# Attention and a GELU feed-forward in one planned kernel: shifted copies on GpSimd, two more bit buffers, new planning tables

## The chip, the cores and the metric

The kernel runs on one core of a Trainium2 chip. The core has five engines with queues of their own: TensorE (PE; its weight loads are shown as PEld), VectorE (DVE), ScalarE (ACT), GpSimd (POOL) and SyncE (SP, which here only issues DMAs). They share the on-chip memory; the matmul results lie in eight banks of their own ("ps"), which GpSimd does not use in this kernel. The metric is the device time of one execution in microseconds (us); lower is better.

## What is computed

A transformer block over 2048 tokens of width 640, in bf16: layer norm, attention with 32 query heads of width 20 that share one key head and one value head, a residual, a second layer norm, a gated feed-forward of width 1536, and a second residual.

```python
q = (x @ wq).reshape(B, S, H, Dh)          # H = 32, Dh = 20
k = x @ wk                                  # one head for all
v = x @ wv
scores = jnp.einsum("bhqd,bkd->bhqk", q, k) * (Dh ** -0.5)
p = softmax(scores)
o = jnp.einsum("bhqk,bkd->bhqd", p, v)
...
h = x + attention(layernorm(x))
y = layernorm(h)
out = h + (gelu(y @ w_gate) * (y @ w_up)) @ w_down
```

## The kernel before, in words

**Tiles and passes.** The tokens are 16 tiles of 128. A tile's 32 heads are done in two halves, so there are 32 passes. A pass needs the scores of 16 heads against 16 key tiles. One *unit* is one key tile against four heads that lie in one quarter of the partitions, a bank of 128 x 512; a pass has 64 units, the kernel 2048. Four units of one key tile make a *quad*.

**Two ways to the exponential.** Most units are done on ScalarE (L979): a group of three or two banks is turned into exponentials in one instruction, written to one of five `pbuf` slots, and multiplied by the values (L1093, `pbuf`, `v_ext`). Some quads of each pass, as many as the digit of `D_QUADS`, are done on VectorE instead. There a "bit product" (L933) adds a bias to the score and writes an integer whose bits, read as bf16, are roughly the exponential. Four such units fill one 2048-wide buffer of `dbuf`. Two further buffers get the same integers plus 43 and plus 85, the *shifted copies* (L944). All three are read as bf16 and multiplied by the values with three weights (L1093, `dbuf`, `v_w`); the sum is close to the true exponential. So a quad on VectorE saves four units on ScalarE, and costs four bit products, two shifted copies, and three value products instead of one. `dbuf` has seven buffers.

**The rest.** Query projections, the output projection, gate, up and down products (all L534, four 32-column strips at once) are spread between the score products (L879). VectorE takes results out of the banks, does layer norms and half of the GELU; GpSimd squares and multiplies for GELU (L1246, L1218; for tiles with a 0 in `Z_POOL` or `H_POOL` VectorE does the product, L1216) and scales the attention output (L1119). ScalarE does one tanh a tile (L1258). Transposes of the normalised input (xnT), the queries (qT), the attention output (onT) and the hidden tile (hhT) are DMAs that SyncE issues.

**What sets the order.** Nothing is decided on the chip. `_Sched.schedule` plans all five queues ahead, with a duration for each task, priorities, and buffer pools; each task is then written out in that order with the waits that the plan implies. Tables with one digit for a pass or tile steer it. Tasks marked `port` on VectorE and GpSimd are planned so that they don't overlap:

```python
if t.port:
    at = max(at, lock[other[e]])
```

**Zero products.** TensorE's clock is granted by its activity, so the plan keeps count of it over a window of 3.42 us (`active`). Where it would be under 1.45 us of array time, a product of zeros with halves is put in front of the next score product (in the profile L534, `halves`, `zeros`). A task's array time is its duration unless `act` says otherwise.

A second program in the file recomputes everything the slow way when a row sum is out of bounds; with these inputs it does not run.

Of the kernel before, what the change touches and what calls it, by code (L numbers as in the profile page):

```python
# [7 lines left out]
BF16 = mybir.dt.bfloat16  # L8
I16 = mybir.dt.int16
F32 = mybir.dt.float32  # L10
P = 128
# [3 lines left out]
class _Slot:  # L15

    __slots__ = ("pool", "index", "left", "want")

# [7 lines left out]
class _Pool:  # L26
# [6 lines left out]
    def slot(self, want=None):  # L33
        return _Slot(self, want)

    def open_for(self, s):
        return [i for i in ((range(len(self.busy))) if s.want is None else (s.want,)) if not self.busy[i]]


class _Task:  # L40
    __slots__ = ("eng", "fn", "dur", "deps", "prio", "acq", "rel", "dma", "name", "start", "end", "seq",
                 "extra", "sem", "val", "needed", "know", "pos", "lag", "cfg", "after", "opens", "rides",
                 "groups", "late", "spare", "held", "act", "hold", "warms", "serve", "phase", "port", "issue")


class _Sched:
# [7 lines left out]

    PATIENCE = "05454444444444443442544443444444"
# [16 lines left out]
    def add(self, eng, fn, dur, deps=(), prio=0.0, acq=(), rel=(), dma=None, name="", lag=0.0,  # L72
            cfg=None, after=(), rides=None, port=False):
        t = _Task()
        t.port = port
        t.issue = 0.08
# [24 lines left out]
        for s in t.rel:  # L101
            s.left += 1
        self.tasks.append(t)
        return t

    def schedule(self):
# [19 lines left out]
        def release(t):  # L126
            at = 0.0
            for d in t.deps + t.after:
                own = d.eng == t.eng and d.dma is None
                hop = (self.OWN[d.eng] if d in t.deps else 0.0) if own else self.HOP[d.eng] + t.lag  # L130
                at = max(at, d.end + hop)
            ready[t.eng].append((at, t))

        def active(a, b):
            return sum((min(y, b) - max(x, a)) / (y - x) * w for x, y, w in busy[-60:] if y > a and x < b)
# [91 lines left out]
        while left:  # L227
            best = None
            for e in self.ENGINES:
                cands = []  # L230
                for at, t in ready[e]:
                    if t.rides and not (cfg == t.cfg and at <= free[e] + 0.02 and t.rides() - groups):
                        at += 0.5 * int(self.PATIENCE[phase])
                    if t.port:
                        at = max(at, lock[other[e]])
                    for s in t.acq:
                        open_ = s.pool.open_for(s)
                        if not open_:
# [17 lines left out]
                if best is None or pick[0] < best[0]:  # L256
                    best = pick
            assert best is not None, ("stuck", [(e, [(t.name, t.prio) for _, t in ready[e]][:6]) for e in ready])
            at, t = best
            e = "pe" if isinstance(t, int) else t.eng  # L260
            if e == "pe" and idle and not isinstance(t, int) and t.warms is not False and (
                    at - free[e] >= self.GAP and active(at - self.WINDOW, at) < self.ACTIVE):
                f = self.add("pe", self.idle[0], self.idle[1], self.idle[2], name="warm", cfg="col")
# [24 lines left out]
            if e == "pe" and opened is not None:  # L288
                c = "col" if isinstance(t, int) else t.cfg
                if t.__class__ is not int and t.cfg == "row" and active(at - self.WINDOW, at) < self.ACTIVE and (  # L290
                        at - free[e] >= self.GAP or active(at - self.WINDOW, at) < self.ACTIVE - .08):
                    fn, dur, deps = self.filler
# [16 lines left out]
            else:  # L309
                ready[e] = [c for c in ready[e] if c[1] is not t]  # L310
                for s in t.acq:
# [3 lines left out]
                    p.busy[i] = True  # L315
                    p.holder[i] = t
                    t.extra += p.users[i]
                    p.users[i] = []
# [100 lines left out]
def bass_sequential_preLN__grouped_kv_mqa__glu_gated_geglu__prompt_kernel(  # L419
# [50 lines left out]
    wd_sb = sb("wd_sb", [P, NF, D])  # L470
    NQB = 3
    q_tok = sb("q_tok", [P, 2, H, 32])
# [12 lines left out]
    mx = sb("mx", [P, 2, 2], F32)  # L485
    onT = sb("onT", [P, 2, ND, P])
    ident = sb("ident", [P, P])
    zeros = sb("zeros", [P, P])
    halves = sb("halves", [P, P])
    halfc = sb("halfc", [P, 1], F32)  # L490
# [30 lines left out]
    XN_pool = _Pool(NXB)  # L521
    ON_pool, OTK_pool = _Pool(1), _Pool(2)
    ONT_pool = _Pool(2)
    QTK_pool, QT_pool = _Pool(2), _Pool(NQB)
    HH_pool = _Pool(2)
    D_pool = _Pool(NDB)
    G_pool = _Pool(2)
# [33 lines left out]

    LAG = "5335334313334532"
    X_LATE = ((8, 12, 14), (9, 14, 16))
# [27 lines left out]
    for a in (4, 8):  # L591
        d = load("sp", xh[:, a:a + 4, :], x_view[:, a:a + 4, :], f"x{a}", 4.2 + a if a == 4 else 9.9)
        for t in range(a, a + 4):
# [14 lines left out]
           for i in range(2)]  # L608
    z_ve = sc.add("pool", lambda e: e.memset(v_ext[:, :, Dh:32], 1.0), 0.3, prio=nprio(), name="z_ve")
    t_zeros = sc.add("dve", lambda e: e.memset(zeros[:], 0.0), 0.2, prio=nprio(), name="zeros")  # L610
    t_halves = sc.add("dve", lambda e: e.memset(halves[:], 0.5), 0.2, prio=nprio(), name="halves")
# [86 lines left out]
    def kv_proj(t):  # L698
# [3 lines left out]
        def fn(e):  # L702
# [4 lines left out]
            for cc in range(ND):  # L707
# [108 lines left out]

    D_QUADS = "05554544444445445444444445453533"
    D_AHEAD = "32222222222224242142522154223222"
    D_BEFORE_END = "33333333333333233331334234343233"
    MARGIN = "22322632235416344511432625366014"  # L820
    MARGIN_2 = "76666666666463366672266626343655"
    D_IN_SET = "11111111111111111111111111111111"
# [45 lines left out]
    d_owed = {p: 3 * len(d_kts[p]) for p in passes}  # L868
    d_quad = {}
    d_terms = {p: [] for p in passes}  # L870
    r_done = {}
# [10 lines left out]
    def stream_d(n, which, set_sl=None):  # L882
# [50 lines left out]
        quad["bits"].append(sc.add("dve", lambda e: e.tensor_scalar(  # L933
            part(seg, w=slice(512 * item[0], 512 * item[0] + 512)), bk(), D_BIAS, 0.0, ALU.add, ALU.max), 0.6, [qk_t],
# [5 lines left out]
        for j in range(3):  # L940
            s, dep = seg, bits
            if j:
                s = D_pool.slot()
                dep = [sc.add("dve", lambda e, j=j, s=s: e.tensor_scalar(part(s), part(seg), D_SHIFT[j], None, ALU.add),  # L944
                              0.602, bits, prio=0.55 * HOT + n * 1e-3, acq=[s], rel=[seg], port=True, name=f"ds{j}_{n}")]
            s.left += 1
# [155 lines left out]

    URGENT = "44535556555555565566542553555655"

# [104 lines left out]

    H_POOL = "1111011111011100"  # L1210
    Z_POOL = "1111111111001100"

# [304 lines left out]
    for e, n in over.items():  # L1517
# [5 lines left out]
    SA_pool, PV_pool, AUX_pool = _Pool(1), _Pool(1), _Pool(2)  # L1523
    LN_pool, XN_pool, ON_pool, ONT_pool, HH_pool, G_pool = (_Pool(4), _Pool(NXB), _Pool(1), _Pool(2), _Pool(2),
                                                            _Pool(2))
    OTK_pool, QTK_pool, QT_pool = _Pool(2), _Pool(2), _Pool(1)
    PR_pool, PT_pool, MX_pool = _Pool(NPB), _Pool(2), _Pool(2)
# [131 lines left out]
```

## Time and profile before

| what | value |
|---|---|
| time, median of 3 runs (lowest to highest) | 758.69 us (757.65 to 760.05) |
| span of the profiled execution | 760.8 us (the page gives no other time of it) |
| ScalarE busy | 729.2 us, 96% |
| TensorE busy | 723.5 us, 95% |
| VectorE busy | 675.4 us, 89% |
| GpSimd busy | 189.8 us, 25% |
| mean granted TensorE clock | 0.987 |

In the profile a row of a group gives the line, the engine, the operation, output and input with shapes, the count, then busy us and the mean length of one in ns, then how long the engine was idle just before and what released it. Neighbouring instructions of an engine overlap a little, so count times mean can be more than the busy time. A row of a stage gives its limits and length, then busy time and count for PE, PEld, DVE, ACT and POOL, the granted clock, the DMA share and GB/s. L numbers are lines of the kernel before; in the changed kernel the same code stands some 55 to 70 lines further down.

### The profile page before, as it was taken

To read this page: it belongs to the slowest core of one execution; us is meant where nothing else is said; L and a number is where in the kernel's file an instruction comes from. 1 tells how busy PE (TensorE), PEld (TensorE's weight loads), DVE (VectorE), ACT (ScalarE), POOL (GpSimd) and SP (SyncE) were. 2 spreads that over 40 slices of the span, in tenths; PEclk is the share of its full clock that TensorE was granted. 3 is DMA by queue.
4 is the path that set the end of the run, shared out by engine and by line. 5 is a ranking of instruction groups with operands and counts; after the bars stand their busy time and mean duration, and the time that the engine had idled before them with its cause. 6 is when DMAs were issued, how large, how long until landed. Compare 5 with 4: busy or idle time off the path is not lost.

```text
span 760.8 us, 23781 instructions
## 1 busy us (share of the span) xinstructions
PE 723.5 (95%) x10601; PEld 262.8 (35%) x10601; DVE 675.4 (89%) x1270; ACT 729.2 (96%) x702; POOL 189.8 (25%) x257
## 2 busy tenths in 40 slices
PE   8888989999999999999999999999999999999997
PEld 3332223333333333333333333333333332323336
DVE  8688999998898898999998988898999999898772
ACT  6898999999999999999999999999999999999972
POOL 6310001151335035102404233140321011250500
PEclk9798999999999999999999999999999999999999
DMA  6793012020111102120110201103021200201020
GB/s 172 136 343 56 17 16 25 3 45 19 24 23 41 33 10 45 21 45 19 22 25 20 45 20 38 27 6 42 19 45 31 36 18 2 48 12 30 14 54 20
DMA packets 80622, 31.67 MB, mean 42 GB/s; under 512 B 71552, under 2 KB 79232, under 8 KB 80512
## 3 DMA queue, kind: packets, MB, share of 16 engines
q1 hardware_dynamic: 79200, 30.03, 18.3%
q8 instruction: 84, 1.38, 0.8%
q10 hardware_dynamic: 1312, 0.05, 0.1%
q14 instruction: 26, 0.21, 0.1%
HBM read 10.21 MB, written 2.62 MB: 17 GB/s over the span
## 4 chain that ended last, share of the span: by engine, by line
ACT 53%; PE 32%; DVE 7%; DMA 5%; POOL 1%; issue 0%
ACT pbuf L979 51%; PE ps L534 12%; PE ps L879 10%; PE ps L1093 8%; DVE dbuf L933 3%; DMA qT<-q_tok 2%; ACT g_z L1258 1%; DVE dbuf L944 1%; DMA xnT<-xn_tmp 1%; PE ps L1378 1%; DMA hhT<-g_us 1%; DVE g_us L1252 1%; DMA onT<-oN 1%; DVE xn_tmp L649 0%; POOL g_z L1218 0%
## 5 line engine op out<-in xcount | busy, mean ns | idle before, releaser
L979 ACT ACTIVATE pbuf<-ps 128x1024 bf16<-128x1024 f32 (+1 forms) x661 | 701.3, 1227 | 8.3 <-PE ps L879 7.4
L933 DVE TENSOR_SCALAR dbuf<-ps 128x512 int16<-128x512 f32 x520 | 341.1, 680 | 38.1 <-PE ps L879 35.3
L879 PE MATMUL ps<-qT,kT 32*128 32x512 bf16 x2048 | 289.4, 387 | 17.6 <-ACT pbuf L979 12.0
L944 DVE TENSOR_SCALAR dbuf<-dbuf 128x2048 int16<-128x2048 int16 x260 | 172.5, 688 | 0.7
L879 PEld LDWEIGHTS ps<-qT,kT 32*128 32x128 bf16 x2048 | 76.2, 91 | 257.0 <-ACT pbuf L979 189.9
L1093 PE MATMUL ps<-pbuf,v_ext 128*32 128x512 bf16 (+3 forms) x2032 | 146.6, 335 | 1.7 <-ACT pbuf L979 1.5
L1093 PE MATMUL ps<-dbuf,v_w 128*32 128x512 bf16 x1560 | 134.8, 384 | 4.5 <-DVE dbuf L933 1.8
L1246 POOL TENSOR_TENSOR g_z<-g_gs 128x512 bf16<-128x512 bf16 x45 | 48.6, 1081 | 131.3 <-DVE g_gs L1244 131.2
L534 PE MATMUL ps<-wd_sb,hhT 128*32 128x320 bf16 x1440 | 68.5, 305 | 0.8 <-DMA hhT<-g_us 0.5
L1093 PEld LDWEIGHTS ps<-pbuf,v_ext 128*32 128x32 bf16 x2032 | 44.4, 94 | 71.7 <-issue 51.5
L534 PE MATMUL ps<-wg_sb,xnT 128*32 128x512 bf16 x900 | 67.9, 383 | 0.7 <-DVE dbuf L933 0.2
L534 PE MATMUL ps<-wu_sb,xnT 128*32 128x512 bf16 x900 | 67.3, 382 | 0.4
L1119 POOL TENSOR_TENSOR oN<-oT,rL 128x320 bf16<-128x320 f32 x30 | 22.1, 738 | 162.9 <-DVE rL L1114 162.6
L1093 PEld LDWEIGHTS ps<-dbuf,v_w 128*32 128x32 bf16 x1560 | 38.6, 95 | 41.1 <-DVE dbuf L944 12.9
L632 POOL CAST lnvb<-mv 128x1 bf16<-128x1 f32 x31 | 7.3, 234 | 171.4 <-DVE mv L630 170.8
L1218 POOL TENSOR_TENSOR g_z<-g_z,g_gs 128x512 bf16<-128x512 bf16 x36 | 41.0, 1166 | 30.6 <-DVE g_z L1255 30.6
L1218 POOL TENSOR_TENSOR g_us<-g_z,g_us 128x512 bf16<-128x512 bf16 x36 | 40.6, 1153 | 24.7 <-DVE g_z L1261 24.7
L534 PEld LDWEIGHTS ps<-wd_sb,hhT 128*32 128x32 bf16 x1440 | 32.1, 96 | 27.5 <-issue 15.9
L1252 DVE SCALAR_TENSOR_TENSOR g_us<-ps,g_gs 128x512 bf16<-128x512 f32 x45 | 30.6, 680 | 4.9 <-PE ps L534 4.7
L534 PE MATMUL ps<-wq_sb,xnT 128*32 128x320 bf16 (+1 forms) x660 | 32.2, 301 | 1.1 <-DVE xnT L682 0.4
L534 PE MATMUL ps<-wo_sb,onT 128*32 128x320 bf16 x600 | 30.5, 302 | 1.5 <-DVE dbuf L933 0.8
L1244 DVE CAST g_gs<-ps 128x512 bf16<-128x512 f32 x45 | 30.4, 675 | 1.7 <-PE ps L534 1.5
(97 smaller groups left out, 363.6 us busy)
## 6 DMA issues: line engine op xcount, KB each, us to landing
out_dram<-xh SPq DMA_DIRECT2D x15, 160.0 KB, 1.8
wg_sb<-in_B_w_gate_dram SPq DMA_DIRECT2D x1, 1920.0 KB, 10.6
wu_sb<-in_B_w_up_dram SPq DMA_DIRECT2D x1, 1920.0 KB, 15.0
wd_sb<-in_B_w_down_dram SPq DMA_DIRECT2D x1, 1920.0 KB, 19.7
xh<-in_A_x_dram SPq DMA_DIRECT2D x2, 640.0 KB, 7.2
xh<-in_A_x_dram SPq DMA_DIRECT2D x3, 320.0 KB, 3.5
wq_sb<-in_A_wq_dram SPq DMA_DIRECT2D x2, 400.0 KB, 4.7
wo_sb<-in_A_wo_dram SPq DMA_DIRECT2D x1, 800.0 KB, 5.3
```

The costliest lines, as they stand in the source:

```text
L534: ins = e.matmul(out[r, :], lhs[:, r], rhs, start=start, stop=stop, tile_position=(0, 32 * b))
L879: return e.matmul(bk.rearrange("p (g n) -> p g n", g=4), kT4[r, kt * P:(kt + 1) * P], qT[r, main_q[t].index, 4 * h:4 * h + 4, :], start=Tr ...
L933: quad["bits"].append(sc.add("dve", lambda e: e.tensor_scalar(part(seg, w=slice(512 * item[0], 512 * item[0] + 512)), bk(), D_BIAS, 0.0, A ...
L944: dep = [sc.add("dve", lambda e, j=j, s=s: e.tensor_scalar(part(s), part(seg), D_SHIFT[j], None, ALU.add), 0.602, bits, prio=0.55 * HOT + ...
L979: exps.append(sc.add("act", lambda e, w0=w0, w1=w1, to=to: e.activation(pbuf[:, to:to + w1 - w0], ps[:, w0:w1], ACT.Exp, scale=EXP_SCALE), ...
L1093: ins = e.matmul(ps[32 * b:32 * b + 32, PVB * 512 + a:PVB * 512 + a + n].rearrange("p (a n) -> p a n", n=32), x[2], span.rearrange("p (a n ...
L1119: onorm[(t, h)] = c = sc.add(by, lambda e: e.tensor_tensor(oN[:, otk.index, h * (D // 2):(h + 1) * (D // 2)].rearrange("p (g l d) -> p l g ...
L1218: return [sc.add("pool", lambda e, c=slice(512 * j, 512 * j + 512): e.tensor_tensor(out[:, k.index, c], a[:, k.index, c], b[:, k.index, c] ...
L1244: ge = sc.add("dve", lambda e, col=col, bk=bk: e.tensor_copy(g_gs[:, gsl.index, col], bk()), d_ps(512), [gm], prio=EVAC + pr, rel=[ax], na ...
L1246: sqt = sc.add("pool", lambda e, col=col: e.tensor_tensor(g_z[:, gsl.index, col], g_gs[:, gsl.index, col], g_gs[:, gsl.index, col], ALU.mult),
L1252: uts.append(sc.add("dve", lambda e, col=col, bk=bk: e.scalar_tensor_tensor(g_us[:, gsl.index, col], bk(), 0.5, g_gs[:, gsl.index, col], A ...
L1258: th = sc.add("act", lambda e: e.activation(g_z[:, gsl.index, :], g_z[:, gsl.index, :], ACT.Tanh, scale=GELU_C), d_act(1536), zt, prio=-5. ...
```

## The change

- A shifted copy may be done on GpSimd, as an addition of 1024 32-bit integers: two 16-bit values at once, plus the shift in both halves. `SHARE` says how many copies of a pass may go there (up to 8); the plan lets GpSimd take one unless VectorE, with what is queued there, would be done with it more than 1 us earlier. The plan's duration for it is 2.25 us.
- `dbuf` gets nine buffers instead of seven. A new pool, `_Quads`, lets a quad begin only while enough buffers are left for the copies of the quads in front of it.
- To make room: two qT buffers (three before), one oN and one onT (two), one hidden tile hhT (two), three `xn_tmp` (four).
- The array time of the key and value products (L706, L708) is counted as 0.33 us in the plan (0.6 before), and the threshold for zero products is now 1.2 + 0.05 x the pass's digit in `FILL` (1.45 for all before).
- New tables: quads by pass (131 in all, 130 before), where in a pass they stand, margins, patience, lags. The copies get another priority. Three more tiles have their z product and one more its h product on VectorE.

```diff
+class _Quads(_Pool):
...
+    def open_for(self, s):
+        spots = [i for i in range(len(self.busy)) if not self.busy[i]]
+        left = [(q, n) for q, n in self.need.items() if n and q != s.quad]
+        keep = 0
+        if s.first:
+            keep = min(left)[1] if left else 2
+        elif left and min(left)[0] < s.quad:
+            keep = min(left)[1]
+        return spots if len(spots) > keep else []
...
-    WINDOW, ACTIVE, GAP = 3.42, 1.45, 0.25
+    WINDOW, GAP = 3.42, 0.25
...
+    SLACK = 1.0
+    FILL = "88383456555577654546654655534555"
...
+                    if e == "pool" and t.other is not None and (
+                            backlog(t, max(at, free[e])) + t.dur + self.SLACK
+                            < max(at, free[e], lock["dve"]) + t.other[1]):
+                        continue
...
+            least = 1.2 + 0.05 * int(self.FILL[phase])
...
-    NQB = 3
+    NQB = 2
...
-    oN = sb("oN", [P, 2, D])
+    oN = sb("oN", [P, 1, D])
...
-    onT = sb("onT", [P, 2, ND, P])
+    onT = sb("onT", [P, 1, ND, P])
...
-    NXB = 4
+    NXB = 3
...
-    hhT = sb("hhT", [P, 2, NF, P])
-    NDB = 7
+    hhT = sb("hhT", [P, 1, NF, P])
+    NDB = 9
...
+        mm.act = 0.33
...
-    D_QUADS = "05554544444445445444444445453533"
...
+    SHARE = "05214322113262221001232432232080"
+    D_QUADS = "05553545454354454534354545453533"
...
+        def pairs(s):
+            return dbuf[:, s.index, :].bitcast(I32)
...
-                s = D_pool.slot()
+                s = D_pool.slot(seg.quad)
...
+                if shared[(t, h)] < int(SHARE[2 * t + h]):
+                    shared[(t, h)] += 1
+                    dep[0].other = (lambda e, j=j, s=s: e.tensor_tensor(
+                        pairs(s), pairs(seg), shifts[:, j - 1:j].to_broadcast([P, 1024]), ALU.add), 2.25)
...
-    H_POOL = "1111011111011100"
-    Z_POOL = "1111111111001100"
+    H_POOL = "1111011111011000"
+    Z_POOL = "0110011111011000"
```

More of the change, by code (lines that the diff above doesn't have):

```diff
@@ L34, in slot, with taken, __init__ @@
         return _Slot(self, want)
+    def taken(self, s):
+        pass
     def open_for(self, s):
         return [i for i in ((range(len(self.busy))) if s.want is None else (s.want,)) if not self.busy[i]]
+class _Quads(_Pool):
+    def __init__(self, n):
+        super().__init__(n)
+        self.need, self.made = {}, 0
+    def slot(self, quad=None):
+        s = _Slot(self)
+        if quad is None:
+            self.made += 1
+            s.quad, s.first = self.made, True
+        else:
+            s.quad, s.first = quad, False
+        return s
+    def open_for(self, s):
[7 more added lines that the diff above has]
+        return spots if len(spots) > keep else []
+    def taken(self, s):
+        if s.first:
+            self.need[s.quad] = 2
+        else:
+            self.need[s.quad] -= 1
 class _Task:
@@ L42 @@
                  "extra", "sem", "val", "needed", "know", "pos", "lag", "cfg", "after", "opens", "rides",
-                 "groups", "late", "spare", "held", "act", "hold", "warms", "serve", "phase", "port", "issue")
+                 "groups", "late", "spare", "held", "act", "hold", "warms", "serve", "phase", "port", "issue", "other")
 class _Sched:
@@ L75, in add @@
         t.port = port
+        t.other = None
         t.issue = 0.08
@@ L132, in release, with backlog @@
             ready[t.eng].append((at, t))
+            if t.other is not None:
+                ready["pool"].append((max(max(d.end + self.HOP[d.eng] for d in t.deps), at - 0.1), t))
+        def backlog(t, now):
+            return max(free["dve"], now) + sum(x.dur for a, x in ready["dve"] if a <= now and x is not t and
+                                               (x.prio, x.seq) < (t.prio, t.seq))
         def active(a, b):
@@ L310, in schedule @@
                 ready[e] = [c for c in ready[e] if c[1] is not t]
+                if t.other is not None:
+                    if e == "pool":
+                        ready[t.eng] = [c for c in ready[t.eng] if c[1] is not t]
+                        t.eng, t.fn, t.dur = e, t.other[0], t.other[1]
+                    else:
+                        ready["pool"] = [c for c in ready["pool"] if c[1] is not t]
                 for s in t.acq:
@@ L869, in bass_sequential_preLN__grouped_kv_mqa__glu_gated_geglu__prompt_kernel @@
     d_quad = {}
+    shared = {p: 0 for p in passes}
     d_terms = {p: [] for p in passes}
```

46 lines of the change are left out of this document (25 added, 21 removed).

## The prediction, made before the run

> **What bounds the kernel now.** I read the page first, then busy time by stage, the groups by line, the waits of ScalarE, the early timelines, and last the chain that ended last.
>
> ```profile
> PE 723.5 (95%) x10601; PEld 262.8 (35%) x10601; DVE 675.4 (89%) x1270; ACT 729.2 (96%) x702; POOL 189.8 (25%) x257
> ...
> ACT 53%; PE 32%; DVE 7%; DMA 5%; POOL 1%; issue 0%
> ...
> L979 ACT ACTIVATE pbuf<-ps 128x1024 bf16<-128x1024 f32 (+1 forms) x661 | 701.3, 1227 | 8.3 <-PE ps L879 7.4
> L933 DVE TENSOR_SCALAR dbuf<-ps 128x512 int16<-128x512 f32 x520 | 341.1, 680 | 38.1 <-PE ps L879 35.3
> L944 DVE TENSOR_SCALAR dbuf<-dbuf 128x2048 int16<-128x2048 int16 x260 | 172.5, 688 | 0.7
> L1093 PE MATMUL ps<-dbuf,v_w 128*32 128x512 bf16 x1560 | 134.8, 384 | 4.5 <-DVE dbuf L933 1.8
> ```
>
> Three engines look full; the stage table (busy us per engine in the order PE, PEld, DVE, ACT, POOL, then the granted TensorE clock) tells which one sets the end.
>
> ```profile
> 0.00:18.50 18.50, 14.92 (x214) 7.08 (x215) 15.10 (x59) 11.59 (x23) 11.40 (x41) 1.00 0.68 175
> 18.50:22.00 3.50, 1.66 (x25) 0.93 (x22) 2.83 (x12) 3.50 (x3) 2.05 (x6) 0.99 0.84 105
> 22.00:32.00 10.00, 9.84 (x89) 4.32 (x89) 6.59 (x27) 7.33 (x7) 4.37 (x14) 0.50 0.69 168
> 32.00:60.00 28.00, 24.97 (x356) 9.99 (x354) 21.51 (x49) 27.38 (x26) 3.18 (x6) 1.00 0.93 274
> 60.00:63.00 3.00, 1.88 (x20) 0.51 (x20) 2.21 (x5) 2.35 (x3) 0.00 (x0) 0.99 0.47 104
> 63.00:69.70 6.70, 6.09 (x49) 1.26 (x49) 4.96 (x8) 5.24 (x5) 0.00 (x0) 0.50 0.01 2
> 120.00:720.00 600.00, 584.30 (x8732) 204.94 (x8731) 552.61 (x985) 598.79 (x566) 160.63 (x181) 1.00 0.14 26
> 738.00:761.00 23.00, 18.82 (x271) 13.31 (x271) 7.67 (x22) 5.48 (x10) 0.55 (x1) 0.93 0.07 21
> ```
>
> From 120 to 720 us ScalarE is idle 600 − 598.79 = 1.2 us, VectorE 47 us. ScalarE's exponentials are the bound, and nothing else can be sped up there. Its 31.6 us of idle (760.8 − 729.2) lie in the start, in two stretches at half clock (2.67 us in 22–32, 1.46 us in 63–69.7), and in the tail behind the last exponential. So the most a change can win is: fewer exponentials, those stretches, the tail.
>
> The exponential takes 1528 units of one head and one key tile (2048 units less 130 quads of 4 done on VectorE): 701.3/1528 = 0.459 us a unit.
>
> **The change, part by part.** The sum is made against the profiled span of 760.8 us; the page gives no other time of that execution. The three runs have their median at 758.69, 2.1 us (0.3%) below, and I carry differences over to it unscaled.
>
> *Quads by pass.* The new table sums to 131 quads where the old one had 130. Its other changes move quads between passes. Four units leave ScalarE: 4 × 0.459 = −1.84 us, all on the bound. VectorE gets four bit products more, 4 × 0.680 = +2.7 us; TensorE three D products more and one value product fewer, about 2 × 134.8/390 = +0.7 us, beside ScalarE.
>
> *Shifted copies on GpSimd.* The table allows 72, but the order of the changed program puts 41 of 262 copies there. VectorE loses 39 copies: 39 × 0.688 = −26.8 us. The price of one on GpSimd (1024 elements, two inputs, 32 bit) has no row; its neighbours are:
>
> ```profile
> L1246 POOL TENSOR_TENSOR g_z<-g_gs 128x512 bf16<-128x512 bf16 x45 | 48.6, 1081 | 131.3 <-DVE g_gs L1244 131.2
> L1218 POOL TENSOR_TENSOR g_z<-g_z,g_gs 128x512 bf16<-128x512 bf16 x36 | 41.0, 1166 | 30.6 <-DVE g_z L1255 30.6
> L1218 POOL TENSOR_TENSOR g_us<-g_z,g_us 128x512 bf16<-128x512 bf16 x36 | 40.6, 1153 | 24.7 <-DVE g_z L1261 24.7
> L1119 POOL TENSOR_TENSOR oN<-oT,rL 128x320 bf16<-128x320 f32 x30 | 22.1, 738 | 162.9 <-DVE rL L1114 162.6
> L1216 DVE TENSOR_TENSOR g_z<-g_z,g_gs 128x1536 bf16<-128x1536 bf16 x3 | 2.9, 954 | 0.1
> L1216 DVE TENSOR_TENSOR g_us<-g_z,g_us 128x1536 bf16<-128x1536 bf16 x3 | 2.9, 952 | 0.0
> ```
>
> The line through 320 elements (738 ns) and 512 (1081 ns) gives 2.0 us; 738 ns scaled by 1024/320 gives 2.4 us; by bytes, from the two-byte row, 4.3 us. The 4-byte row beside the 2-byte row costs no more per element, so I take 2.2 us: 41 × 2.2 = +90 us on GpSimd.
>
> *GELU products.* Three tiles' z products and one tile's h product go from GpSimd to VectorE: 3 × 0.954 + 0.952 = +3.8 us on VectorE, −(9 × 1.166 + 3 × 1.153) = −14 us on GpSimd. VectorE's balance is −26.8 + 2.7 + 3.8 = −20.3 us, GpSimd's +76 us (to 266 us, 35%). All of VectorE's gain is hidden behind ScalarE at 99.8%: I count it 0. It would count only where VectorE holds back a QK product, and ScalarE's idle from 120 to 720 us is 1.2 us in all.
>
> *The shared way to the memory.* Two copies on VectorE take 1.29 us at 731.63, but here 2.05:
>
> ```profile
> 501.24 2.05 DVE L944 TENSOR_SCALAR dbuf<-dbuf 128x2048 int16<-128x2048 int16 x2
> ...
> 501.09 1.05 POOL L1246 TENSOR_TENSOR g_z<-g_gs 128x512 bf16<-128x512 bf16 x1
> ...
> 731.63 1.29 DVE L944 TENSOR_SCALAR dbuf<-dbuf 128x2048 int16<-128x2048 int16 x2
> ```
>
> The copy started while GpSimd worked and ended only after it: 0.76 us lost. The plan keeps such pairs apart, so few occur; a GpSimd copy of 2.2 us could hold one for about twice as long. Behind a held copy stand the bit products of L933, which free the banks that the next QK products need. The Trainium skill, Advanced Engine Details and Errata, VectorE Performance Modes, says that GpSimd's instructions and VectorE's two-port modes block each other; the trace agrees (0.76 us). By this rule the move has a price on VectorE that the −26.8 us above leave out; the last but one rival below works it out from rows. Bounds for the middle stage: −1.2 us (its whole idle goes) and +10 us (the rival below). I take +0.5, near what the plan reached before.
>
> *Fewer buffers elsewhere.* Two more bit buffers are paid for with one transposed hidden tile, one oN and onT, two qT, three xn_tmp. The last matters at the start: a normalise now waits for the transpose three tiles earlier. The late transpose issued at 17.86 is tile 7's; its buffer is next wanted by tile 10, whose normalise began at 23.60.
>
> ```profile
> 17.86 4.25 DMA xnT<-xn_tmp
> 22.16 0.71 PE ps L706 x5
> ...
> 23.60 0.45 DVE L649 TENSOR_SCALAR xn_tmp<-xh,mv,lnr 128x640 bf16<-128x640 bf16 x1
> ```
>
> It landed at 22.11, so this wait costs 0. A transpose of the hidden tile now waits in SyncE's queue for the down products of the tile before; behind it stand the q, onT and output DMAs. The closest pair, tiles 4 and 5, has 26 units between its tanhs: 11.9 us, against a landing of 3.7 us and down products of 68.5/15 = 4.6 us.
>
> ```profile
> hhT<-g_us SPq DMA_TRANSPOSE x15, 3.7
> ...
> L534 PE MATMUL ps<-wd_sb,hhT 128*32 128x320 bf16 x1440 | 68.5, 305 | 0.8 <-DMA hhT<-g_us 0.5
> ```
>
> It fits, cost 0; the number of SyncE's DMAs is the same. If a queue slips, +2 us.
>
> *Zero products and the clock.* The plan now counts the K/V products at 0.33 us of array time, not 0.6, and its threshold for zero products varies by pass. It places 13 groups more: eight more in the first three passes, one fewer in the fourth, six more after that. Zero groups fill TensorE's gaps, but ahead of a QK product that ScalarE waits for they cost. What ScalarE lost in these stretches:
>
> ```profile
> 23.59 1.02 ACT L979 ACTIVATE pbuf<-ps 128x1024 bf16<-128x1024 f32 x1 [1.46 <-PE ps L879]
> 25.11 4.77 ACT L979 ACTIVATE pbuf<-ps 128x1536 bf16<-128x1536 f32 x4 [0.50 <-PE ps L879]
> 30.35 1.45 ACT L979 ACTIVATE pbuf<-ps 128x1536 bf16<-128x1536 f32 x1 [0.47 <-PE ps L879]
> 32.42 4.71 ACT L979 ACTIVATE pbuf<-ps 128x1024 bf16<-128x1024 f32 x4 [0.62 <-PE ps L879]
> ...
> 14.32 0.45 PE L706 MATMUL ps<-xnT,wk 128*128 128x128 bf16 x5
> 22.16 0.71 PE L706 MATMUL ps<-xnT,wk 128*128 128x128 bf16 x5 [1.84 <-DMA xnT<-xn_tmp]
> ```
>
> Of the 1.46 us some 0.5 are the half clock (K/V products 0.71 against 0.45 us, the QK products alike); the rest is the late DMA and stays. Recoverable: 0.5 + 0.50 + 0.47 + 0.62 = 2.1 us. In the new order two zero products stand ahead of 18.5 us and none in the part of pass 0 where TensorE was idle before the drop (18.5–22: 1.66 of 3.5 us busy); the next come just behind it. They can shorten the stretch, hardly prevent it: I take −1.0, between 0 and −2.1, and add +0.8 if they only delay QK products. For 63–69.7 no new zero product stands in the idle part before it (60–63) either, but the work of passes 1 and 2 is shuffled: −0.5, between 0 and −1.46. The tail (738–761) has a mean clock of 0.93, so 2 × 0.07 × 23 = 3.2 us of it at half clock, worth at most 1.6. Behind ScalarE's last tanh now come 10 units where 12 came, so the last hidden tile lands 0.9 us later against the end. I take 0, between −1.6 and +1.
>
> **Sum**: −1.84 + 0.5 − 1.0 − 0.5 = −2.84 us, 758.69 − 2.84 = 755.85.
>
> **Rivals.**
> *The clock stays as it is.* Only the exponentials go: −1.84 + 0.5 = −1.3, 757.4. For it: the gap before 22 us comes from a DMA that landed late, which no plan saw. Against: eight new groups in three passes. The Trainium skill, TensorE: Matmul & The Clock Gate, Part 1, says that the activity window is 3413 ns long and runs free of the kernel; by that zero products placed by a plan can miss it. The half-clock stretches, 0.50 in the stage table, lie where low activity went before, as that would have it.
>
> *All stretches go*: −1.84 − 2.1 − 1.46 − 1.6 = −7.0, 751.7. Against it stands where the zero products are.
>
> *GpSimd holds VectorE* (slower). If half of the 41 copies meet a VectorE copy and each lets ScalarE wait once for a mean wait of 7.4/15 = 0.49 us, the middle costs 20 × 0.49 = +9.8:
>
> ```profile
> ACT pbuf L979 <- PE ps L879: 7.4, 15, 1.5
> ```
>
> 755.85 + 9.3 (for the 0.5 already in) = 765.2. It turns the sign from six such waits (2.84/0.49). For it: the 0.76 us above, and GpSimd's longest instruction doubles. Against: the plan locks both engines against each other, and VectorE has 20 us more room.
>
> *A tighter buffer slips*: about +2 for one late hidden tile or q tile, 757.9 to 760.
>
> **How the numbers follow.** A measurement of this kernel tells about 0.3% (2.3 us) from no change. Forecast 0.48 (its own range 753 to 757), clock stays 0.22, all stretches go 0.10, GpSimd holds 0.12, a buffer slips 0.08. Faster: 0.43 + 0.10 = 0.53. Same: 0.05 + 0.22 + 0.03 = 0.30; slower 0.12 + 0.05 = 0.17. The range 751 to 762 leaves out most of the GpSimd case and part of the buffer case on one side and a little of the largest gain on the other.
>
> **What would show it.** Right: ScalarE's exponentials near 699.5 us in 659 instructions, its idle from 120 to 720 us near 2 us; the copies at 2.0 to 2.4 us on GpSimd; VectorE near 655 us; a half-clock stretch near 22 us shorter than 10 us. Wrong: VectorE copies of over 1.4 us in number, or QK waits of ScalarE in the middle above 4 us in sum, or GpSimd copies of 4 us; or a half-clock stretch in a new place.

## The result: 2.2% slower

The changed kernel takes 774.76 us (median of 4 runs, 774.31 to 775.04); the kernel before took 758.53 us beside it (757.65 to 760.05). The ratio is 1.0221, with a 95% interval of 1.0202 to 1.0240 (the two medians alone would give 1.0214). Forecast were 755.85 us and a range of 751 to 762.

The profiled execution of the changed kernel spans 773.5 us, 12.7 us more than the one before. The profiled execution before was itself a long one: its 760.8 us of span are more than any of those four whole runs took. Accounts by traces therefore reach 12.7 us, and the medians 16.2 us.

The page of the changed kernel gives busy time by engine, the chain that ended last, and the groups:

```profile
PE 728.5 (94%) x10625; PEld 262.2 (34%) x10625; DVE 672.4 (87%) x1239; ACT 728.9 (94%) x700; POOL 263.1 (34%) x288
...
ACT 39%; PE 37%; DVE 17%; DMA 5%; POOL 1%; issue 1%
...
L1048 ACT ACTIVATE pbuf<-ps 128x1024 bf16<-128x1024 f32 (+1 forms) x659 | 701.0, 1217 | 21.1 <-PE ps L942 20.5
L998 DVE TENSOR_SCALAR dbuf<-ps 128x512 int16<-128x512 f32 x524 | 344.6, 682 | 48.6 <-PE ps L942 46.3
...
L1009 DVE TENSOR_SCALAR dbuf<-dbuf 128x2048 int16<-128x2048 int16 x221 | 158.1, 737 | 0.7
...
L1162 PE MATMUL ps<-dbuf,v_w 128*32 128x512 bf16 x1572 | 138.7, 386 | 8.7 <-DVE dbuf L1009 6.8
L1013 POOL TENSOR_TENSOR dbuf<-dbuf,shifts 128x1024 int32<-128x1024 int32 x41 | 81.9, 2002 | 73.9 <-DVE dbuf L998 73.9
```

(L1048 answers to L979 before, L998 to L933, L1009 to L944, L1162 to L1093, L942 to L879, and L592 to L534.) ScalarE's exponentials are as busy as before, 701.0 us against 701.3, but ScalarE is idle for 21.1 us in front of them where it was 8.3. The 12.8 us of difference are the whole difference of the spans. VectorE shows up in the chain with 17%, 7% before. Its copies have a longer mean, 737 ns against 688, and TensorE now waits 6.8 us for them (1.3 before).

The stages (columns as in the prediction) tell where ScalarE's new idle time lies:

```profile
18.50:22.00 3.50, 0.98 (x15) 0.66 (x14) 1.61 (x8) 2.33 (x2) 1.94 (x6) 0.95 1.01 85
22.00:32.00 10.00, 10.00 (x114) 4.55 (x111) 7.71 (x30) 7.70 (x7) 3.32 (x11) 0.68 0.77 167
56.00:68.00 12.00, 7.82 (x73) 1.76 (x65) 6.67 (x11) 6.74 (x7) 0.00 (x0) 0.72 0.40 82
...
120.00:720.00 600.00, 579.91 (x8658) 202.72 (x8650) 544.82 (x951) 590.55 (x557) 216.83 (x202) 0.99 0.14 27
160.00:200.00 40.00, 36.46 (x520) 13.22 (x521) 35.45 (x59) 34.70 (x34) 16.36 (x14) 0.91 0.12 28
```

From 120 to 720 us it is idle 9.5 us, where it was 1.2; more than half of that, 5.3 us, lies between 160 and 200 us. From 56 to 68 us it is idle 5.3 us. In the kernel before, the same two stretches read:

```profile
56.00:68.00 12.00, 10.11 (x107) 2.38 (x107) 10.19 (x17) 10.42 (x10) 0.00 (x0) 0.79 0.52 107
160.00:200.00 40.00, 39.31 (x608) 13.74 (x604) 33.42 (x60) 39.87 (x38) 13.74 (x14) 1.00 0.09 20
```

The two places have different causes. At 181 us the timeline (start, length, engine, what it did, idle time before) shows two copies on VectorE and two on GpSimd at the same time:

```profile
181.35 4.68 DVE L1009 TENSOR_SCALAR dbuf<-dbuf 128x2048 int16<-128x2048 int16 x2
...
181.16 4.32 POOL L1013 TENSOR_TENSOR dbuf<-dbuf,shifts 128x1024 int32<-128x1024 int32 x2 [1.26 <-DVE dbuf L998]
...
183.79 0.40 PE L1162 MATMUL ps<-dbuf,v_w 128*32 128x512 bf16 x4 [1.63 <-DVE dbuf L1009]
...
186.09 0.62 PE L1162 MATMUL ps<-dbuf,v_w 128*32 128x512 bf16 x4 [1.03 <-DVE dbuf L1009]
...
185.10 1.02 ACT L1048 ACTIVATE pbuf<-ps 128x1024 bf16<-128x1024 f32 x1 [1.59 <-PE ps L942]
187.82 1.02 ACT L1048 ACTIVATE pbuf<-ps 128x1024 bf16<-128x1024 f32 x1 [1.70 <-PE ps L942]
```

The pair on VectorE took 4.68 us; the pair without GpSimd took 1.29 (the prediction's row at 731.63). TensorE goes by its planned order: it stood twice in front of value products whose copy was late, the next score products stood behind these, and ScalarE ran out of banks. TensorE was idle 2.6 us of these 4.7, and from 185.5 us on the granted clock is half for 6.8 us, a stretch that the kernel before doesn't have.

At 57 us it is a DMA. TensorE's and ScalarE's timelines, and SyncE's:

```profile
60.68 0.60 PE L942 MATMUL ps<-qT,kT 32*128 32x512 bf16 x1 [3.86 <-DMA qT<-q_tok]
...
62.84 1.02 ACT L1048 ACTIVATE pbuf<-ps 128x1024 bf16<-128x1024 f32 x1 [4.63 <-PE ps L942]
```

```profile
38.52 0.50 SPq L641 DMA_DIRECT2D wo_sb<-in_A_wo_dram  x1
39.06 0.53 SPq L641 DMA_DIRECT2D wg_sb<-in_B_w_gate_dram  x1
39.63 0.53 SPq L641 DMA_DIRECT2D wu_sb<-in_B_w_up_dram  x1
40.20 2.18 SPq L641 DMA_DIRECT2D wd_sb<-in_B_w_down_dram  x1
42.46 13.95 SPq L814 DMA_TRANSPOSE qT<-q_tok  x1
```

The transposed queries of tile 1 were issued at 42.46 us behind four weight loads, and landed some 18 us later. The kernel before has the same queue, but TensorE came for these queries only at 59.9 us (56.8 in the changed kernel) and waited 1.0 us:

```profile
60.95 0.37 PE L879 MATMUL ps<-qT,kT 32*128 32x512 bf16 x1 [1.01 <-DMA qT<-q_tok]
```

What brought TensorE there 3 us sooner is a digit of a table that the prediction doesn't mention: `D_AHEAD`, which says how far ahead of a pass its first quad on VectorE begins. For pass 2, the first one of tile 1, it went from 2 to 4.

So there were two theories. **Held copies**: GpSimd's copies hold VectorE's copies, one instruction at a time, and this costs about 7 us. **Late queries**: pass 2 starts too early for the transpose, and this costs about 5 us. The rivals were that the order by the new tables is worse in itself, and that the smaller buffers cost.

### The profile page after: what moved, and what is told of

It reads as the page before. It is cut to its first block, busy times and chain, and to the rows that moved or that the text cites. A ratio compares the mean times of both kernels' runs of the same rounds, so it can differ in the third digit from the quotient of the medians.

```text
span 773.5 us, 23819 instructions
## 1 busy us (share of the span) xinstructions
PE 728.5 (94%) x10625; PEld 262.2 (34%) x10625; DVE 672.4 (87%) x1239; ACT 728.9 (94%) x700; POOL 263.1 (34%) x288
## 4 chain that ended last, share of the span: by engine, by line
ACT 39%; PE 37%; DVE 17%; DMA 5%; POOL 1%; issue 1%
ACT pbuf L1048 37%; PE ps L942 13%; PE ps L592 12%; PE ps L1162 10%; DVE dbuf L998 7%; DVE dbuf L1009 5%; DMA qT<-q_tok 2%; ACT g_z L1327 1%; DMA hhT<-g_us 1%; PE ps L1447 1%; DVE oT L1181 1%; DMA xnT<-xn_tmp 1%; DVE g_gs L1313 1%; DVE g_us L1321 1%; DVE stats L686 1%
## 5 line engine op out<-in xcount | busy, mean ns | idle before, releaser
L1048 ACT ACTIVATE pbuf<-ps 128x1024 bf16<-128x1024 f32 (+1 forms) x659 | 701.0, 1217 | 21.1 <-PE ps L942 20.5
L998 DVE TENSOR_SCALAR dbuf<-ps 128x512 int16<-128x512 f32 x524 | 344.6, 682 | 48.6 <-PE ps L942 46.3
L942 PE MATMUL ps<-qT,kT 32*128 32x512 bf16 x2048 | 288.7, 388 | 20.3 <-ACT pbuf L1048 11.0
L942 PEld LDWEIGHTS ps<-qT,kT 32*128 32x128 bf16 x2048 | 75.1, 91 | 261.9 <-ACT pbuf L1048 177.5
L1009 DVE TENSOR_SCALAR dbuf<-dbuf 128x2048 int16<-128x2048 int16 x221 | 158.1, 737 | 0.7
L1162 PE MATMUL ps<-pbuf,v_ext 128*32 128x512 bf16 (+3 forms) x1992 | 146.2, 338 | 2.9 <-ACT pbuf L1048 1.9
L1162 PE MATMUL ps<-dbuf,v_w 128*32 128x512 bf16 x1572 | 138.7, 386 | 8.7 <-DVE dbuf L1009 6.8
L1013 POOL TENSOR_TENSOR dbuf<-dbuf,shifts 128x1024 int32<-128x1024 int32 x41 | 81.9, 2002 | 73.9 <-DVE dbuf L998 73.9
L1315 POOL TENSOR_TENSOR g_z<-g_gs 128x512 bf16<-128x512 bf16 x45 | 50.7, 1127 | 115.5 <-DVE g_gs L1313 114.4
L592 PE MATMUL ps<-wg_sb,xnT 128*32 128x512 bf16 x900 | 69.4, 383 | 1.6 <-DVE dbuf L998 1.2
L592 PE MATMUL ps<-wd_sb,hhT 128*32 128x320 bf16 x1440 | 69.1, 306 | 0.7 <-DMA hhT<-g_us 0.4
L1162 PEld LDWEIGHTS ps<-pbuf,v_ext 128*32 128x32 bf16 x1992 | 44.0, 95 | 70.5 <-issue 51.3
L592 PE MATMUL ps<-wu_sb,xnT 128*32 128x512 bf16 x900 | 67.6, 383 | 0.0
L1162 PEld LDWEIGHTS ps<-dbuf,v_w 128*32 128x32 bf16 x1572 | 39.4, 96 | 48.6 <-DVE dbuf L1009 16.6
L692 POOL CAST lnvb<-mv 128x1 bf16<-128x1 f32 x31 | 8.9, 286 | 117.3 <-DVE mv L690 116.8
L1287 POOL TENSOR_TENSOR g_us<-g_z,g_us 128x512 bf16<-128x512 bf16 x33 | 37.7, 1167 | 30.2 <-DVE g_z L1330 30.2
L592 PEld LDWEIGHTS ps<-wd_sb,hhT 128*32 128x32 bf16 x1440 | 32.6, 97 | 25.5 <-issue 14.1
L1287 POOL TENSOR_TENSOR g_z<-g_z,g_gs 128x512 bf16<-128x512 bf16 x27 | 30.6, 1157 | 25.1 <-DVE g_z L1324 25.1
L592 PE MATMUL ps<-wq_sb,xnT 128*32 128x320 bf16 (+1 forms) x660 | 32.7, 297 | 1.4 <-DVE xnT L742 0.4
```

The source lines that it names most:

```text
L592: ins = e.matmul(out[r, :], lhs[:, r], rhs, start=start, stop=stop, tile_position=(0, 32 * b))
L942: return e.matmul(bk.rearrange("p (g n) -> p g n", g=4), kT4[r, kt * P:(kt + 1) * P], qT[r, main_q[t].index, 4 * h:4 * h + 4, :], start=Tr ...
L1013: dep[0].other = (lambda e, j=j, s=s: e.tensor_tensor(pairs(s), pairs(seg), shifts[:, j - 1:j].to_broadcast([P, 1024]), ALU.add), 2.25)
L1048: exps.append(sc.add("act", lambda e, w0=w0, w1=w1, to=to: e.activation(pbuf[:, to:to + w1 - w0], ps[:, w0:w1], ACT.Exp, scale=EXP_SCALE), ...
L1162: ins = e.matmul(ps[32 * b:32 * b + 32, PVB * 512 + a:PVB * 512 + a + n].rearrange("p (a n) -> p a n", n=32), x[2], span.rearrange("p (a n ...
L1287: return [sc.add("pool", lambda e, c=slice(512 * j, 512 * j + 512): e.tensor_tensor(out[:, k.index, c], a[:, k.index, c], b[:, k.index, c] ...
```

## Experiments

The kernels ran in two groups, each with the kernel before beside it: 758.27 us for the cut copies, the four pieces, the moved loads and the kernel without shared copies, 759.51 us for the others. I compare ratios to the kernel before; 0.1% is 0.76 us.

### Each copy on GpSimd cut short

From the third tile on, a copy on GpSimd writes 128 of its 1024 pairs. This leaves out part of the shifted copies, and with them part of the exponentials' sum. The order of all queues is that of the changed kernel.

```diff
-                    dep[0].other = (lambda e, j=j, s=s: e.tensor_tensor(
-                        pairs(s), pairs(seg), shifts[:, j - 1:j].to_broadcast([P, 1024]), ALU.add), 2.25)
+                    w = 1024 if t < 2 else 128
+                    dep[0].other = (lambda e, j=j, s=s, w=w: e.tensor_tensor(
+                        pairs(s)[:, 0:w], pairs(seg)[:, 0:w], shifts[:, j - 1:j].to_broadcast([P, w]), ALU.add), 2.25)
```

> The changed kernel, its order on all engines as it is; only the shifted copies that GpSimd makes from tile 2 on (36 of 41) write 128 of their 1024 pairs, so each lasts some 0.3 us and not 1.9. Their buffers then hold old data in the rest: part of the sum of those quads is left out. Theory 1 (GpSimd's long copies hold VectorE's two-port copies, and through the bit products and the score products ScalarE): the held VectorE copies from 160 us on (14 of over 0.75 us in the whole run, 11.7 us too long in sum, 2 of them in the first 75 us) all but vanish, the stretch of 5.3 us idle at 167 to 193 us and the 1.5 us at 590 go, the time falls by 6 to 9 us, to 766 to 769. Theory 2 (the late query transpose of tile 1 is the main cost) expects the same 774.8, within 1. Theory 3 (the plan itself: fewer buffers, tables, zero products) also expects 774 to 775.

769.74 us, ratio 1.0157 (1.0127 to 1.0187): 4.9 us of the loss are gone. The group of the copies, and the waits of ScalarE:

```profile
L1014 POOL TENSOR_TENSOR dbuf<-dbuf,shifts 128x128 int32<-128x128 int32 (+1 forms) x41 | 29.7, 727 | 76.6 <-DVE dbuf L998 76.5
```

```profile
ACT pbuf L1049 <- PE ps L942: 14.0, 18, 4.6
```

The waits in front of exponentials fall from 20.5 to 14.0 us, and those near 184 and at 590 us are gone. The 4.6 us at 57 us stay, and so does one of 1.57 us at 71.5 us, where the copies were left whole. So the length of GpSimd's copies is a cause, and the wait at 57 us has another.

One expectation was missed: the held copies on VectorE don't all but vanish. 12 of the 14 stay, together 6.7 us too long instead of 11.7. In the changed kernel only six of the 14 stand beside a copy on GpSimd, and they are 7.3 us too long (four and 2.3 us in this run). The other eight, 4.4 us, stand beside a GELU product of GpSimd (L1315 and L1287; L1246 and L1218 before), and these eight are the same in this run. One of them in the changed kernel, whose second copy ends 0.55 us after the product:

```profile
417.84 2.13 DVE L1009 TENSOR_SCALAR dbuf<-dbuf 128x2048 int16<-128x2048 int16 x2
418.00 1.42 POOL L1315 TENSOR_TENSOR g_z<-g_gs 128x512 bf16<-128x512 bf16 x1 [4.53 <-DVE g_gs L1313]
```

### The same copies in four pieces

Nothing is left out; each copy on GpSimd is four additions of 256 pairs. The order is again the same.

```diff
-                    dep[0].other = (lambda e, j=j, s=s: e.tensor_tensor(
-                        pairs(s), pairs(seg), shifts[:, j - 1:j].to_broadcast([P, 1024]), ALU.add), 2.25)
+                    dep[0].other = (lambda e, j=j, s=s: [e.tensor_tensor(
+                        pairs(s)[:, a:a + 256], pairs(seg)[:, a:a + 256], shifts[:, j - 1:j].to_broadcast([P, 256]),
+                        ALU.add) for a in range(0, 1024, 256)][-1], 2.25)
```

> The changed kernel, order unchanged; each shifted copy on GpSimd is made in four instructions of 256 pairs. Theory 1a (what hurts is how long one GpSimd instruction keeps VectorE out): a held copy loses at most some 0.6 us, the time falls by 3 to 8 us, to 767 to 772. Theory 1b (what hurts is the whole time in which GpSimd uses the way to the memory): no gain, 774 to 776, as VectorE's copy loses to each piece in turn. Theories 2 and 3: 774 to 775 and perhaps 1 more for the added instructions.

767.27 us, ratio 1.0121 (1.0104 to 1.0138): 7.6 us less than the changed kernel. The group of the copies, and the timeline at the place that took 4.68 us:

```profile
L1013 POOL TENSOR_TENSOR dbuf<-dbuf,shifts 128x256 int32<-128x256 int32 x164 | 101.9, 654 | 72.3 <-DVE dbuf L998 72.3
```

```profile
179.66 2.12 DVE L1009 TENSOR_SCALAR dbuf<-dbuf 128x2048 int16<-128x2048 int16 x2
...
179.47 5.63 POOL L1013 TENSOR_TENSOR dbuf<-dbuf,shifts 128x256 int32<-128x256 int32 x8 [1.26 <-DVE dbuf L998]
```

GpSimd works 20 us longer on its copies (101.9 us against 81.9) and the kernel is faster. The pair on VectorE takes 2.12 us now: VectorE gets in after a piece. Total work on GpSimd, or the traffic that it makes, would have gone the other way. What costs is that one GpSimd instruction holds a VectorE copy to its end. The six copies on VectorE that stand beside a copy on GpSimd are 2.0 us too long now, 7.3 in the changed kernel, and the half-clock stretch at 185.5 us is gone; the eight beside GELU products stay at 4.4 us. That this run gains more than the one before fits the copies of the first two tiles, which were whole there and are in pieces here: the wait at 71.5 us is down to 0.29 us. But the intervals of the two runs overlap.

### The queries of tile 1 ahead of the weight loads

```diff
-    after_T = [x for t in range(8, NT) for x in ln1_T[t]]
+    after_T = [x for t in range(8, NT) for x in ln1_T[t]] + [q_evicted[(1, 0)], q_evicted[(1, 1)]]
```

This moves the four loads on SyncE behind that transpose; all other queues keep their order.

> The changed kernel, order unchanged on all engines but SyncE, where the four weight loads (wo, wg, wu, wd, 6.5 MB) are issued behind the query transpose of tile 1 and not ahead of it. Theory 2 (the transpose lands at 60.7 us because the loads stand before it, and the new table wants it 4.3 us sooner): TensorE's 3.9 us wait and ScalarE's 4.6 us idle at 58 us go, and the half clock behind it; the time falls by 4 to 6 us, to 769 to 771. Theory 1 gives this place no part: within 1 us of 774.8 only if the time is made good elsewhere. If the weights come too late, a new wait stands near 100 us.

770.02 us, ratio 1.0159 (1.0136 to 1.0182): 4.7 us less. The DMA's view, the stage and the waits:

```profile
DMA to landing us min/median/max: 2.5/3.0/3.9
```

```profile
56.00:68.00 12.00, 9.50 (x118) 2.83 (x114) 11.80 (x17) 11.13 (x11) 3.59 (x2) 0.98 0.86 288
```

```profile
ACT pbuf L1048 <- PE ps L942: 14.9, 23, 2.4
```

In the changed kernel the same DMA view reads

```profile
DMA to landing us min/median/max: 2.5/3.0/18.2
```

so the late landing came from the loads in front of it. From 56 to 68 us ScalarE gains 4.4 us (11.13 against 6.74), and the clock is 0.98 there instead of 0.72. Not all of the half clock is gone: 3.4 us of it begin at 67.5 us, and ScalarE waits 2.4 us at 69.5, behind a copy on VectorE that a whole copy on GpSimd holds (2.38 us from 64.9 on).

### Both cures together

> The changed kernel with both edits: copies on GpSimd in four pieces, weight loads behind the query transpose. If theories 1a and 2 hold and add up: 774.8 - 5 - 5 = 762 to 767. If 1b holds: 769 to 771, as the loads alone.

The kernel with both edits takes 763.15 us, ratio 1.0044 (1.0022 to 1.0065). Of the 1.77% that separate the changed kernel from this, the two edits alone give 1.00% and 0.62%: they add up within the intervals, so the two causes are separate. The middle stage and the start, and then the waits:

```profile
120.00:720.00 600.00, 582.53 (x8716) 203.99 (x8708) 544.16 (x955) 596.07 (x562) 234.36 (x304) 1.00 0.14 28
...
18.50:34.00 15.50, 12.99 (x124) 5.67 (x121) 9.49 (x38) 10.87 (x9) 6.44 (x21) 0.56 0.83 134
```

```profile
ACT pbuf L1049 <- PE ps L942: 9.9, 21, 2.4
```

0.44%, or 3.3 us, are left against the kernel before. From 120 to 720 us ScalarE is idle 3.9 us (1.2 before), in many small waits; from 18.5 to 34 us it is busy 10.87 us, where the kernel before has

```profile
18.50:34.00 15.50, 13.49 (x147) 6.28 (x148) 10.84 (x45) 12.41 (x11) 7.04 (x21) 0.67 0.66 138
```

The stretch at the start doesn't need the tables for a cause. In the changed kernel, whose order is the same up to there, ScalarE is busy 12.04 us in it at a clock of 0.78, here 10.87 at 0.56: it differs that much between executions of one order. In the middle the eight copies held by GELU products are still there, 4.4 us too long. Whether these make the small waits, or which of the new tables does, is open; the tables act on one plan, and a single one was not undone in the changed kernel.

### No shared copies at all

```diff
-    SHARE = "05214322113262221001232432232080"
+    SHARE = "00000000000000000000000000000000"
```

> The changed kernel planned anew with no shifted copy on GpSimd (SHARE all 0); buffers, tables, zero products as changed. VectorE gets 41 copies back, about 28 us of work. Theory 1: no held copies beyond those of the kernel before, the time falls by 5 to 10 us, to 765 to 770, unless VectorE, now at 700 us, holds up TensorE instead. Theory 3: 774 or more, as the tables were made for shared copies. Theory 2: its 4 us stay in.

786.39 us, ratio 1.0373 (1.0352 to 1.0394): a miss. With all copies on VectorE the plan becomes another one:

```profile
ACT pbuf L1048 <- PE ps L942: 15.2, 19, 4.1
ACT pbuf L1048 <- PE ps L1162: 9.6, 4, 5.5
```

The first row is the known wait; in the second, ScalarE waits for value products that free its output slots, four times and up to 5.5 us, which neither kernel has. The new tables rest on the shared copies, so this run doesn't price the copies; it shows only that the new tables are worse without them.

### The loads moved in the kernel before

The same edit of `after_T` in the kernel before; only SyncE's order changes.

> The kernel before, order unchanged but on SyncE, where the four weight loads are issued behind the query transpose of tile 1. Theory 2: the kernel before has the same fault in small (ScalarE idle 0.65 us at 61.6, then a half-clock stretch with 1.46 us); both go, the time falls by 1.5 to 2.5 us, to 756 to 757. Rival: the loads then lie under other transposes and cost what they gave, 758 to 759.

757.64 us (12 runs) against 759.51, ratio 0.9978 (0.9960 to 0.9997). This is the lowest median of the study, and the interval just leaves out 1. Its row from 56 to 72 us, and then the one of the kernel before:

```profile
56.00:72.00 16.00, 14.57 (x187) 4.54 (x191) 15.93 (x29) 16.00 (x17) 0.73 (x1) 1.00 0.76 211
```

```profile
56.00:72.00 16.00, 14.11 (x153) 3.58 (x153) 13.17 (x23) 13.72 (x13) 0.73 (x1) 0.79 0.39 81
```

ScalarE has no gap left there and the half-clock stretch at 63 us is gone. The prediction hoped that the shuffled work of passes 1 and 2 would shorten that stretch; here it went with the late transpose in front of it. One trace can't show that it stays away, since it comes in some executions and not in others (the last experiment has one without it). But 11 of these 12 runs lie below the median of the kernel before, 759.51 us. A query transpose lands late here too, 19.3 us after its issue at 47.5 us, now behind the loads; no score product waits for it.

### The earlier start of pass 2 alone, in the kernel before

```diff
-    D_AHEAD = "32222222222224242142522154223222"
+    D_AHEAD = "32422222222224242142522154223222"
```

> The kernel before with one table digit changed, the cycles by which the first VectorE scores of tile 1 stand ahead of its pass: 4 as in the changed kernel, 2 before. Theory 2: TensorE then wants the query transpose 4 to 5 us sooner, waits near 4 us for it at 57 to 61 us, and the time rises by 3 to 5 us, to 762 to 764. Rival (the wait is covered): 758 to 760.

761.17 us, ratio 1.0020 (1.0004 to 1.0036): +1.5 us by the ratio, where 3 to 5 were expected, and near the lower end of what can be told from no change. In the stretch from 50 to 70 us the waits are

```profile
ACT pbuf L979 <- PE ps L879: 4.5, 2, 4.3
...
PE ps L879 <- DMA qT<-q_tok: 3.6, 1, 3.6
```

so the one digit makes the wait that the changed kernel shows (3.86 and 4.63 us). It costs less than that, probably because the kernel before already loses time at the same place: 0.65 us of wait, and 1.46 us at half clock in the profiled execution. From 56 to 72 us ScalarE is busy 11.43 us here and 13.72 there.

### The smaller buffers alone, in the kernel before

Seven bit buffers as before, but the smaller pools of the change:

```diff
-    NQB = 3
+    NQB = 2
...
-    oN = sb("oN", [P, 2, D])
+    oN = sb("oN", [P, 1, D])
...
-    onT = sb("onT", [P, 2, ND, P])
+    onT = sb("onT", [P, 1, ND, P])
-    NXB = 4
+    NXB = 3
-    hhT = sb("hhT", [P, 2, NF, P])
+    hhT = sb("hhT", [P, 1, NF, P])
```

> The kernel before with only the smaller buffers of the change (two qT, one oN, one onT, one hhT, three xn_tmp), still seven bit buffers. Its planned order is nearly the same. Theory 3 in its form 'the buffers cost': 760 to 763. Theories 1 and 2: no change, 758 to 759.5.

759.21 us, ratio 1.0010 (0.9990 to 1.0030): nothing that can be measured. VectorE does wait now:

```profile
21.49 0.45 DVE L649 TENSOR_SCALAR xn_tmp<-xh,mv,lnr 128x640 bf16<-128x640 bf16 x1 [1.78 <-DMA xnT<-xn_tmp]
```

and ScalarE's eleventh exponential starts at 25.39 us instead of 25.11. That is too little to be seen in the time. This execution had no half clock between 56 and 72 us, so that stretch comes in some executions and not in others; the profiled one of the kernel before had it.

## Why the prediction was wrong

**The shared way to the memory: this step failed.** The prediction took +0.5 us, since the plan "keeps such pairs apart, so few occur". The plan does so on paper; on the chip nothing enforces it, and the timeline shows both at work at once. In the trace 14 of the 221 copies on VectorE took over 0.75 us and were together 11.7 us too long against the median of 0.685 us (4 copies and 1.4 us before). Of this, 7.3 us stand beside copies on GpSimd. The four pieces won 7.6 us of time back, the half-clock stretch behind the longest hold included. The other 4.4 us stand beside GELU products, which the new order lets meet VectorE's copies more often than the old one; what these cost wasn't tried. The rival "GpSimd holds VectorE" had the mechanism and nearly the size (+9.8 us), but the wrong picture: not twenty waits of 0.49 us, but a few large ones, which also cost the clock once. Its evidence stood in the prediction, a copy pair that a 1.05-us GpSimd instruction had stretched by 0.76 us, and the chance of 0.12 was too low for it. "A GpSimd copy of 2.2 us could hold one for about twice as long" was right (the longest copy took 2.38 us, 1.7 too long); that most of 41 such copies went into a stage where ScalarE had 1.2 us to spare should have weighed more than the plan's lock. The Trainium skill's rule that the prediction named (Advanced Engine Details and Errata, VectorE Performance Modes), that GpSimd's instructions and VectorE's two-port modes block each other, is what the trace shows: 4.68 us against 1.29.

**Where a pass's quads begin: a term that was missing.** The prediction priced the quads' number and not where they stand (`D_AHEAD`). The earlier start of pass 2 ran into a DMA whose landing stood in the trace of before, with a wait of 1.0 us on it. Moving the loads won 4.7 us. This was settled by following the one wait of a score product for a DMA, and no view of the middle stage could show it.

**Quads by pass: the size held, the gain didn't.** 659 exponentials came as forecast, and four units fewer. But busy time fell by 0.3 us, not by 1.84. The sum took ScalarE's busy time as work that can be saved; the last section shows that it contains waits. That most of the units' gain went there is read from the traces and wasn't tried by itself.

**The copies' price: right.** 41 copies at 2.00 us were forecast at 2.2, and GpSimd's total is 263.1 us (266 forecast). VectorE's total is another matter: 672.4 us instead of 655, and the held copies are 11.7 us of the 17.

**Fewer buffers: the time was right, one step not.** The normalise that takes a third buffer again does wait for the late transpose,

```profile
21.81 0.45 DVE L709 TENSOR_SCALAR xn_tmp<-xh,mv,lnr 128x640 bf16<-128x640 bf16 x1 [1.89 <-DMA xnT<-xn_tmp]
```

where the prediction had put that off to a later tile at 23.60. In the kernel before, with the smaller buffers, the same wait cost no time that could be measured (ratio 1.0010). In the changed kernel it wasn't taken away.

**The clock: half right, and that half may be luck.** The stretch from 22 us on was shorter, 6.8 us instead of 10.2 (granted clock from 22 to 32 us 0.68 instead of 0.50). But it differs between executions of one order. From 18.5 to 34 us the clock is 0.78 in the changed kernel and 0.89, 0.89, 0.67 and 0.56 in the four runs with its order up to there (cut copies, four pieces, moved loads, both cures); in the kernel before it is 0.67, and 0.57 with the loads moved. So these traces don't show that the zero products shortened it. ScalarE gained only 0.4 us in that stage, and lost 1.2 us just before it (busy 2.33 of 3.5 us, 3.50 before). The stretch at 63 us came earlier, at 59.2, and a new one came at 185.5. Both follow an idle TensorE, one behind a DMA and one behind held copies, and no zero product stands in either idle part. "A half-clock stretch in a new place" was named as a sign of being wrong.

**The tail: right.** From the end of the last exponential to the end of the span it is 22.8 us before and 22.9 us after.

The sum by what was measured: +7.6 for the held copies, +4.7 for the late queries, and 3.3 us that stay with both cures. That makes 15.6 of the 16.8 us by which the ratio puts the kernel behind. The remaining 1.2 us are within the intervals of the runs. What makes the 3.3 us is open.

## What to carry to other kernels

Work that leaves an engine with time to spare for a helper is not free because the helper is idle: if the two exclude each other, the price can be the length of one helper instruction in front of whatever waits for the first engine. So look for the helper's longest single instructions, all of them and not only the new ones, and cut them into pieces before counting totals. When a table moves work to an earlier time, follow each of its inputs back to the DMA that brings it, and to what stands in front of that DMA on its queue.

## What the runs showed that I had not expected

**Busy time of ScalarE contains waits.** The groups of exponentials of the kernel before, kept apart by shape:

```profile
L979 ACT ACTIVATE pbuf<-ps 128x1024 bf16<-128x1024 f32 x455 | 456.5, 1095 | 5.1 <-PE ps L879 4.4
L979 ACT ACTIVATE pbuf<-ps 128x1536 bf16<-128x1536 f32 x206 | 312.5, 1517 | 3.2 <-PE ps L879 3.0
```

455 × 1.095 + 206 × 1.517 = 811 us, against 701.3 us in which ScalarE is busy: successive instructions overlap in the records. The starts of exponentials that follow each other without a gap lie 0.904 us apart behind one of two banks and 1.330 us behind one of three. By that all of them need 455 × 0.904 + 206 × 1.330 = 685.3 us, and 683.5 us after the change (453 and 206). The rest of the busy time, 16.0 us before and 17.5 us after, is for the most part single starts that come late while the end of the instruction before still counts as busy: by the records of starts and ends 11.0 us in 110 places before and 12.0 us in 119 after. Each of these starts comes within 0.05 us of the end of a score product, so they are waits. So "ScalarE is idle 1.2 us from 120 to 720 us" was no proof that nothing could be won or lost there, and of the 1.8 us that the four units save, 1.5 went into this rest, about 1 of it into more late starts; 0.3 us is what the busy time shows.

**The hold works in both directions, and for tiny instructions.** While VectorE did three copies in a row from 177.36 us, two GpSimd instructions on 128x1 took 0.53 and 1.11 us:

```profile
177.36 1.84 DVE L1009 TENSOR_SCALAR dbuf<-dbuf 128x2048 int16<-128x2048 int16 x3
...
177.51 0.53 POOL L692 CAST lnvb<-mv 128x1 bf16<-128x1 f32 x1 [6.96 <-DVE mv L690]
178.13 1.11 POOL L694 TENSOR_SCALAR lnve<-lnvb 128x1 bf16<-128x1 bf16 x1
```

Their medians are 0.19 and 0.23 us. They stand on GpSimd ahead of the two copies at 181.16 us. That this delay is what made those copies meet VectorE's is likely from the order, but wasn't tried.

**Four pieces cost a quarter more.** A copy in one piece has a mean of 2.00 us and in four 4 × 0.654 = 2.6 us as they are recorded, 101.9/41 = 2.5 us by busy time; the fixed part of a GpSimd addition is thus about (2.5 − 2.0)/3 = 0.16 us, an estimate from these rows, which contain holds too.
